# Attention units: the steps of a unit's division spread over ten pairs, a fourth buffer for its sums, routed rows gathered two units ahead, and conversions of `wo` and of the output taken in two pieces

## The chip, the cores and the metric

The kernel runs on one core of a Trainium2 chip. The metric is the device time of one execution in microseconds; the median of 3 runs before the change is 1352.32 us (1351.72 to 1353.39). Engine names are those of the profile: PE (matmuls), PEld (its weight loads), ACT, DVE, POOL, and SP, which here only issues DMAs.

## What is computed

The output is a gated mix of two branches over the same 2048 tokens of width 448: a 16-head attention without a mask (head width 28), and a mixture of 8 experts of which each token takes the best two.

```python
x = A_x
g = _sigmoid((x * gate_w).sum(-1, keepdims=True))
a = _A_ref(x, A_wqkv, A_wo)
b = _B_ref(x, B_w_gate, B_w1, B_w2)
return g * a + (1 - g) * b
```

`_A_ref` is softmax(q k / sqrt(28)) v for each head, then a product with `wo`. `_B_ref` adds, for each expert, its gate weight times silu(x w1) w2.

## The kernel before

The kernel has three stages. The first (to about 116 us of the span) computes q, k, v and the routing. The second (to about 835 us) runs the experts and writes each routed row to the DRAM tensor `ys_d`; PE also takes the row maxima of the scores there. The third, which the change touches, is the attention, followed by the product with `wo`.

The attention runs in 16 units (`NU`): a unit `u` is a group `g` of 4 heads and a block `qc` of 512 queries, `u = 4 g + qc`. A unit is 8 pairs (`NPR`), a pair being two tiles of 128 keys; `m = 8 u + p` counts pairs, 0 to 127. The main loop issues for each `m`, in this order, `scores(m + 1)`, `beside(m)` and `values(m)`. PE, ACT, DVE and POOL run in exactly the order of the code; the DMAs of SP are put in order by a scheduler.

- `scores(m)` takes the scores of a pair on PE into 8 banks of PSUM: for each key tile three heads in a triple `s` and one in a single `z`. ACT turns them into `P` with four exponentials: of the first `z` (L1173), of the first triple (L1174), of the second triple (L1176), and of `X` (L1177), a copy of the second `z` that DVE makes (L1175) so that the bank is free early.
- `values(m)` multiplies `P` with `V` on PE (L1188, 16 matmuls) into a single `z`. DVE adds that to the unit's accumulator `osb` (L1194; at `p == 0` it is a copy, L1192).
- The two singles are used in turn: `values(m)` writes the bank that `scores(m + 1)` used for its first tile, so it waits for L1173; and the last head of the second tile of `scores(m + 2)` goes into the bank of `values(m)`, so PE waits there for DVE's copy or add of `values(m)` into `osb`.
- `beside(m)` holds what is put between the two, and its DVE work stands between the copy `X` of pair `m + 1` and the `osb` step of pair `m`:

```python
        if p in (2, 4, 5, 6):
            next(sums.setdefault(u, routed(u)))
```

  `routed(t)` mixes the two expert rows of each of 128 tokens into `b1`, in four DVE steps (L1073 twice, L1075, L1077); the rows come by `fetch_routed(t)`, two gathers (L1064) that POOL issues, each of 128 rows of 3,584 bytes from `ys_d`. A unit's division (the softmax sums are row 28 of each head in `osb`) takes five steps over DRAM: `collect_sums` (5 DMAs of POOL, the last of which reads the sums back in another layout), `invert_sums` (a reciprocal of DVE and a DMA), `spread_sums` (4 DMAs), `divide` (a DVE product, L1127, and 4 to 8 DMAs of SP into `OT`, L1137). Before, they stand in the next unit at `p` = 0, 3, 4 and 7. In units 4 to 8 the weights `wo` are loaded and converted by `split_wo`; in unit 15 `split_o` converts three tiles of `OT` on DVE (L1086, L180, L181).

After the loop come 16 tiles of the product with `wo` (L1097), each finished by DVE (L1100) and stored by SP; the last unit's division runs beside them.

Of the kernel before, what the change touches and what calls it, by code (L numbers as in the profile page):

```python
# [8 lines left out]
F32 = mybir.dt.float32  # L9
F32R = mybir.dt.float32r  # L10
BF = mybir.dt.bfloat16
I32 = mybir.dt.int32
AF = mybir.ActivationFunctionType
ALU = mybir.AluOpType
# [48 lines left out]
def tile_gated_mha_moe(ctx: ExitStack, tc: tile.TileContext, x, xe_, xT, wv, wqk, wo, w1, w2, out):  # L63
    nc = tc.nc
# [673 lines left out]
    with ExitStack() as pb:  # L738
# [161 lines left out]
        for e in range(E):  # L900
# [12 lines left out]
            for hf in range(2):  # L913
# [75 lines left out]
                for n_k, k in enumerate((4, 0, 1, 2, 3)):  # L989
# [11 lines left out]
                    i = 0  # L1001
# [50 lines left out]
        wo_r[b] = sb.tile([128, D], F32, name="wo_r")  # L1052
        nc.sync.dma_start(wo_r[b], wo[:, b])

    def split_wo(b):
        w_ = wo_r[b]
        nc.vector.tensor_copy(wo_h[:, b], w_)
        nc.vector.tensor_tensor(wo_l[:, b], w_, wo_h[:, b].bitcast(F32), op=ALU.subtract)

    def fetch_routed(t):  # L1060
        yg = []
# [7 lines left out]
    def routed(t):  # L1069
# [7 lines left out]
        nc.vector.scalar_tensor_tensor(b1, yg[1][:, 0], coef[:, 2, t:t + 1], b1, op0=ALU.mult, op1=ALU.add)  # L1077
        yield

    def split_o(t, eng):  # L1080
        ts = slice(t * 128, (t + 1) * 128)
        oh = sb.tile([128, 4, 128], F32R, name="oh", bufs=4)
        if eng is nc.scalar:
            nc.scalar.activation(oh, OT[:, :, ts], AF.Copy)
        else:
            nc.vector.tensor_copy(oh, OT[:, :, ts])  # L1086
        ol = sb.tile([128, 3, 128], F32R, name="ol", bufs=4)
        split_xl(OT[:, :, ts], oh, ol, 128)
        halves[t] = (oh, ol)

    def project(pa_, oh, ol, cs=slice(0, D)):
        mms = []
# [15 lines left out]
    def collect_sums(u):  # L1108
        for j in range(4):
            nc.gpsimd.dma_start(sum_d[u, j:j + 1], accs[u][32 * j + DH:32 * j + DH + 1])  # L1110
        rc[u] = sb.tile([128, 16], F32, name="rc")
        nc.gpsimd.dma_start(rc[u], by_slices(sum_d[u]))

# [66 lines left out]
    def values(m):  # L1180
        u, p = divmod(m, NPR)
        P = Pc.pop(m)
        po = single(m + 1)
        for i in range(2):
            kt = 2 * p + i
            v = held[u // 4][1][kt // 8]
            for j in range(4):
                nc.tensor.matmul(po[32 * j:32 * j + 32], v[:, kt % 8, 32 * j:32 * j + 32], P[4 * i + j],  # L1188
                                 start=i == 0, stop=i == 1)
        if p == 0:  # L1190
            accs[u] = sb.tile([128, 512], F32, name="osb", bufs=3)
            nc.vector.tensor_copy(accs[u], po)  # L1192
        else:
            nc.vector.tensor_tensor(accs[u], po, accs[u], op=ALU.add)  # L1194

    def beside(m):
        u, p = divmod(m, NPR)
        g, qc = divmod(u, 4)
        if qc == 3 and g + 1 < NG:
            if p == 3:  # L1200
                held[g + 1] = [load_k(g + 1, 0), None], [None, None]
            if p == 4:
                held[g + 1][1][0] = load_v(g + 1, 0)
            if p == 6:
                held[g + 1][0][1] = load_k(g + 1, 1)
        if g and qc == 0 and p == 0:
            held[g][1][1] = load_v(g, 1)
        if u and p == 0:
            collect_sums(u - 1)
        if p == 5 and u + 1 < NU:  # L1210
            fetch_routed(u + 1)
        if p == 4 and 4 <= u < 8:
            fetch_wo(u - 4)
        if p == 0 and 5 <= u < 9:
            split_wo(u - 5)
        if (u, p) in WHOLE_O:
            split_o(WHOLE_O.index((u, p)), nc.vector)
        if u and p == 3:
            invert_sums(u - 1)
        if u and p == 4:  # L1220
            spread_sums(u - 1)
        if u and p == 7:
            divide(u - 1)
        if p in (2, 4, 5, 6):
            next(sums.setdefault(u, routed(u)))

    fetch_routed(0)
    WHOLE_O = [(NU - 1, 0), (NU - 1, 1), (NU - 1, 3)]
    for m in range(NU * NPR):
        if m + 1 < NU * NPR:  # L1230
            scores(m + 1)
        beside(m)
        values(m)
    collect_sums(NU - 1)
    split_o(3, nc.scalar)

    for t in range(NT):
# [66 lines left out]
```

## Time and profile before

| | us |
|---|---|
| median of 3 runs | 1352.32 |
| lowest, highest | 1351.72, 1353.39 |
| profiled execution | 1347.44 |
| its span, first to last instruction | 1345.60 |
| attention, first exponential (L1173) to the end of the last values | 835.92 to 1305.9 |
| of it, one pair in the steady part | 3.69 |

The profiled execution is 4.9 us below the median; 1.84 us of it lie outside its span. In the timeline rows each line gives the start, the duration, the engine, the line of the code, the operation with its tiles, how many instructions are merged, and in brackets the idle time of the engine before it and what ended that. ACT starts an instruction before the one ahead of it has ended, so its rate is read from ends (start plus duration), not from durations.

### The profile page before, as it was taken

The page shows a single profiled execution, that of the slowest core. Times are in us where ns is not written, and L with a number is a line of the kernel's source. Part 1 is how long each engine was busy: PE and PEld are TensorE (multiplying, and loading weights), DVE is VectorE, ACT ScalarE, POOL GpSimd, SP SyncE. Part 2 cuts the span into 40 slices and gives each one's busy share as a digit, 9 for nine tenths or more (in the row PEclk, how much of TensorE's full clock was granted, in tenths as well). Part 3 has the DMA queues.
Part 4 walks back from the last instruction along what each step waited for, and adds up shares of the span by engine and source line. Part 5 has one row for each costly group of instructions (what it writes and reads, how often), then busy time and mean ns, then how long its engine had stood idle before and what let it go on. Part 6 is the DMA issues. An engine that isn't in the chain of part 4 may idle for free. (4 is left out here: it accounts for less than half of the span.)

```text
span 1345.6 us, 27214 instructions
## 1 busy us (share of the span) xinstructions
PE 1339.2 (100%) x10166; PEld 888.0 (66%) x10166; DVE 927.7 (69%) x1076; ACT 847.5 (63%) x1270; POOL 617.1 (46%) x661
## 2 busy tenths in 40 slices
PE   9999999999999999999999999999999999999998
PEld 8888788788887777777777777444444444444448
DVE  5736898888988888988898785444454544444465
ACT  5325354364354343543445535999999999999981
POOL 2123765676587577775777753122222222222220
PEclk9999999999999999999999999999999999999999
DMA  9887856753553465534655303223422422342213
GB/s 354 300 266 269 301 154 196 242 153 107 159 157 95 146 201 154 149 101 143 204 156 152 105 36 93 64 58 103 126 83 72 130 80 58 101 126 74 59 31 129
DMA packets 136278, 191.30 MB, mean 142 GB/s; under 512 B 23284, under 2 KB 102680, under 8 KB 135632
## 3 DMA queue, kind: packets, MB, share of 16 engines
q1 hardware_dynamic: 124992, 160.55, 38.6%
q0 software_dynamic: 11008, 28.76, 7.2%
q8 instruction: 80, 1.31, 0.4%
q14 instruction: 54, 0.44, 0.1%
q10 hardware_dynamic: 144, 0.23, 0.1%
HBM read 139.20 MB, written 60.74 MB: 149 GB/s over the span
## 5 line engine op out<-in xcount | busy, mean ns | idle before, releaser
L143 DVE TENSOR_REDUCE mp<-pm 128x3 f32<-128x1536 f32 (+1 forms) x301 | 508.9, 1733 | 11.0 <-PE pm L122 11.0
L1188 PE MATMUL z<-P,V 128*32 128x512 f32 x2032 | 244.7, 598 | 0.1
L1176 ACT ACTIVATE P<-s 128x1536 f32<-128x1536 f32 x127 | 199.2, 1568 | 0.0
L1174 ACT ACTIVATE P<-s 128x1536 f32<-128x1536 f32 x127 | 197.6, 1556 | 0.0
L1175 DVE COPY X<-z 128x512 f32<-128x512 f32 x127 | 87.9, 692 | 150.7 <-PE z L733 141.5
L733 PE MATMUL s<-Q,Kh 29*128 29x512 f32 x1524 | 187.7, 444 | 0.0
L733 PE MATMUL z<-Q,Kh 29*128 29x512 f32 x508 | 185.6, 444 | 0.0
L804 POOL TENSOR_TENSOR w2l<-w2r,w2h 128x448 fp32r<-128x448 f32 x112 | 129.4, 1156 | 119.2 <-ACT w2h L798 80.1
L1020 ACT ACTIVATE yo<-acc 128x448 f32<-128x448 f32 x64 | 34.9, 546 | 233.2 <-PE acc L1006 228.8
L1006 PE MATMUL acc<-w2h,hh 128*128 128x448 f32 x448 | 167.6, 374 | 0.3 <-PEq L818 0.3
L1006 PE MATMUL acc<-w2h,hl 128*128 128x448 f32 x448 | 166.5, 372 | 0.0
L1006 PE MATMUL acc<-w2l,hh 128*128 128x448 f32 x448 | 166.1, 371 | 0.0
L949 ACT ACTIVATE hf<-acc 128x512 f32<-128x512 f32 (+6 forms) x154 | 74.3, 482 | 137.9 <-PE acc L945 131.1
L136 DVE TENSOR_REDUCE mp<-acc 128x1 f32<-128x512 f32 x130 | 89.5, 688 | 85.0 <-PE pm L122 83.1
L813 POOL TENSOR_TENSOR hl<-hf,hh 128x512 fp32r<-128x512 f32 x112 | 145.1, 1295 | 1.0 <-ACT hh L952 1.0
L733 PEld LDWEIGHTS z<-Q,Kh 29*128 29x128 f32 x508 | 74.5, 183 | 106.5 <-DVE yg L1073 26.8
L1188 PEld LDWEIGHTS z<-P,V 128*32 128x32 f32 x2032 | 53.1, 109 | 130.1 <-issue 76.0
L945 PE MATMUL acc<-xeh,w1h 128*128 128x512 f32 (+3 forms) x408 | 136.8, 339 | 0.0
L1194 DVE TENSOR_TENSOR osb<-z,osb 128x512 f32<-128x512 f32 x112 | 77.4, 691 | 85.7 <-PE z L1188 85.6
L945 PE MATMUL acc<-xeh,w1l 128*128 128x512 f32 (+3 forms) x408 | 136.0, 338 | 0.0
L772 POOL TENSOR_TENSOR w1l<-w1r,w1h 128x1024 fp32r<-128x1024 f32 (+1 forms) x49 | 90.8, 1853 | 60.8 <-ACT w1h L766 47.1
L122 PE MATMUL pm<-khg,qg 28*128 28x512 f32 x894 | 110.5, 449 | 0.9 <-DVE lo L645 0.9
(221 smaller groups left out, 2704.7 us busy)
## 6 DMA issues: line engine op xcount, KB each, us to landing
w2r<-in_w_dram SPq DMA_DIRECT2D x112, 224.0 KB
w1r<-in_w_dram SPq DMA_DIRECT2D x56, 384.0 KB
ys_d<-zero_d SPq DMA_DIRECT2D x32, 448.0 KB
ys_d<-yo SPq DMA_DIRECT2D x64, 224.0 KB
x_d<-xf SPq DMA_DIRECT2D x115, 64.0 KB
qkh_d<-hi SPq DMA_DIRECT2D x28, 256.0 KB
qkl_d<-lo SPq DMA_DIRECT2D x28, 256.0 KB
w1r<-in_w_dram SPq DMA_DIRECT2D x112, 64.0 KB
```

The source lines that it names most:

```text
L122: nc.tensor.matmul(banks[n], qgs[g, qt // 4][rw, (qt % 4) * 128:(qt % 4 + 1) * 128], kh[g, kc][rw], start=True, stop=True)
L136: nc.vector.tensor_reduce(mp[:, o:o + 1], banks[0], axis=AX.X, op=ALU.max)
L143: nc.vector.tensor_reduce(mp[:, (o + lo) % 256:(o + lo) % 256 + hi - lo], pm[h][:, lo - 3 * h:hi - 3 * h], axis=AX.X, op=ALU.max)
L733: nc.tensor.matmul(banks[j], k[rw, ks], q[rw, c], start=i == 0, stop=i == 2)
L772: nc.gpsimd.tensor_tensor(l[:, :, half], r[:, :, half], h[:, :, half].bitcast(F32), op=ALU.subtract)
L804: nc.gpsimd.tensor_tensor(w2l, w2r, w2h.bitcast(F32), op=ALU.subtract)
L813: nc.gpsimd.tensor_tensor(hl, hf32, hh[:, 0:512].bitcast(F32), op=ALU.subtract)
L945: nc.tensor.matmul(pu[:, 0:HC], a, b[:, cs], start=i == 0, stop=i == len(mms) - 1)
L1006: nc.tensor.matmul(py[:n, 0:D], a[:, cs], b, start=i == 0, stop=i == 3 * NH - 1)
L1174: nc.scalar.activation(P[:, 1:4], t[0], AF.Exp, scale=SCALE)
L1176: nc.scalar.activation(P[:, 4:7], t[1], AF.Exp, scale=SCALE)
L1188: nc.tensor.matmul(po[32 * j:32 * j + 32], v[:, kt % 8, 32 * j:32 * j + 32], P[4 * i + j], start=i == 0, stop=i == 1)
```

## The change

Of a unit's division, reading the sums back becomes a step of its own (`slice_sums`) at `p == 2` of the next unit, `invert_sums` stays at `p == 3`, `spread_sums` moves to `p == 5`, and `divide` to `p == 2` of the unit after that, so that the division of unit 14 stands behind the loop; `osb` gets 4 buffers instead of 3. `routed(t)` is worked off one unit earlier (at `p` 4 to 7 of unit `t - 1`), for unit 0 at `p` 0 to 3 of unit 0 itself; the gathers of units 0 and 1 are issued ahead of the loop and then those of `u + 2` at `p == 4`. `split_wo` is divided into a rounding at `p == 0` and a subtraction at `p == 1`, and the three `split_o` of unit 15 into two parts each, at `p` 0 and 1, 4 and 5, 6 and 7.

```diff
--- before.py
+++ after.py
@@ -1052,10 +1052,11 @@
         wo_r[b] = sb.tile([128, D], F32, name="wo_r")
         nc.sync.dma_start(wo_r[b], wo[:, b])
 
-    def split_wo(b):
-        w_ = wo_r[b]
-        nc.vector.tensor_copy(wo_h[:, b], w_)
-        nc.vector.tensor_tensor(wo_l[:, b], w_, wo_h[:, b].bitcast(F32), op=ALU.subtract)
+    def split_wo_high(b):
+        nc.vector.tensor_copy(wo_h[:, b], wo_r[b])
+
+    def split_wo_low(b):
+        nc.vector.tensor_tensor(wo_l[:, b], wo_r.pop(b), wo_h[:, b].bitcast(F32), op=ALU.subtract)
 
     def fetch_routed(t):
         yg = []
@@ -1077,16 +1078,19 @@
         nc.vector.scalar_tensor_tensor(b1, yg[1][:, 0], coef[:, 2, t:t + 1], b1, op0=ALU.mult, op1=ALU.add)
         yield
 
+    def split_o_high(t, eng):
+        halves[t] = oh, ol = sb.tile([128, 4, 128], F32R, name="oh", bufs=4), sb.tile([128, 3, 128], F32R, name="ol", bufs=4)
+        if eng is nc.scalar:
+            nc.scalar.activation(oh, OT[:, :, t * 128:(t + 1) * 128], AF.Copy)
+        else:
+            nc.vector.tensor_copy(oh, OT[:, :, t * 128:(t + 1) * 128])
+
+    def split_o_low(t):
+        split_xl(OT[:, :, t * 128:(t + 1) * 128], *halves[t], 128)
+
     def split_o(t, eng):
-        ts = slice(t * 128, (t + 1) * 128)
-        oh = sb.tile([128, 4, 128], F32R, name="oh", bufs=4)
-        if eng is nc.scalar:
-            nc.scalar.activation(oh, OT[:, :, ts], AF.Copy)
-        else:
-            nc.vector.tensor_copy(oh, OT[:, :, ts])
-        ol = sb.tile([128, 3, 128], F32R, name="ol", bufs=4)
-        split_xl(OT[:, :, ts], oh, ol, 128)
-        halves[t] = (oh, ol)
+        split_o_high(t, eng)
+        split_o_low(t)
 
     def project(pa_, oh, ol, cs=slice(0, D)):
         mms = []
@@ -1108,6 +1112,8 @@
     def collect_sums(u):
         for j in range(4):
             nc.gpsimd.dma_start(sum_d[u, j:j + 1], accs[u][32 * j + DH:32 * j + DH + 1])
+
+    def slice_sums(u):
         rc[u] = sb.tile([128, 16], F32, name="rc")
         nc.gpsimd.dma_start(rc[u], by_slices(sum_d[u]))
 
@@ -1188,7 +1194,7 @@
                 nc.tensor.matmul(po[32 * j:32 * j + 32], v[:, kt % 8, 32 * j:32 * j + 32], P[4 * i + j],
                                  start=i == 0, stop=i == 1)
         if p == 0:
-            accs[u] = sb.tile([128, 512], F32, name="osb", bufs=3)
+            accs[u] = sb.tile([128, 512], F32, name="osb", bufs=4)
             nc.vector.tensor_copy(accs[u], po)
         else:
             nc.vector.tensor_tensor(accs[u], po, accs[u], op=ALU.add)
@@ -1207,31 +1213,45 @@
             held[g][1][1] = load_v(g, 1)
         if u and p == 0:
             collect_sums(u - 1)
-        if p == 5 and u + 1 < NU:
-            fetch_routed(u + 1)
+        if u and p == 2:
+            slice_sums(u - 1)
+        if p == 4 and u + 2 < NU:
+            fetch_routed(u + 2)
         if p == 4 and 4 <= u < 8:
             fetch_wo(u - 4)
         if p == 0 and 5 <= u < 9:
-            split_wo(u - 5)
-        if (u, p) in WHOLE_O:
-            split_o(WHOLE_O.index((u, p)), nc.vector)
+            split_wo_high(u - 5)
+        if p == 1 and 5 <= u < 9:
+            split_wo_low(u - 5)
+        if u > 1 and p == 2:
+            divide(u - 2)
         if u and p == 3:
             invert_sums(u - 1)
-        if u and p == 4:
+        if u and p == 5:
             spread_sums(u - 1)
-        if u and p == 7:
-            divide(u - 1)
-        if p in (2, 4, 5, 6):
-            next(sums.setdefault(u, routed(u)))
+        if u == 0 and p < 4:
+            next(first)
+        if p > 3 and u + 1 < NU:
+            next(sums.setdefault(u, routed(u + 1)))
+        if u == NU - 1 and p in AT_O:
+            i = AT_O.index(p)
+            if i % 2:
+                split_o_low(i // 2)
+            else:
+                split_o_high(i // 2, nc.vector)
 
     fetch_routed(0)
-    WHOLE_O = [(NU - 1, 0), (NU - 1, 1), (NU - 1, 3)]
+    fetch_routed(1)
+    first = routed(0)
+    AT_O = (0, 1, 4, 5, 6, 7)
     for m in range(NU * NPR):
         if m + 1 < NU * NPR:
             scores(m + 1)
         beside(m)
         values(m)
     collect_sums(NU - 1)
+    slice_sums(NU - 1)
+    divide(NU - 2)
     split_o(3, nc.scalar)
 
     for t in range(NT):
```

Two places on DVE and one on SP show what moves. DVE at the start of the attention, before (`X`: the copy of the second single, `osb`: the step behind `values`, `yg`: a gathered tile, whose first sum is L1073, L1074 after the change):

```order
L1175 COPY X<-z_9818 128x512
L1192 COPY osb<-z_9837 128x512
L1175 COPY X<-z_9864 128x512
L1194 TENSOR_TENSOR osb<-z_9883,osb 128x512
L1175 COPY X<-z_9909 128x512
L1073 TENSOR_TENSOR yg_9798<-yg_9798 128x448
L1194 TENSOR_TENSOR osb<-z_9930,osb 128x512
```

The same place after the change:

```order
L1181 COPY X<-z_9822 128x512
L1074 TENSOR_TENSOR yg_9798<-yg_9798 128x448
L1198 COPY osb<-z_9843 128x512
L1181 COPY X<-z_9870 128x512
L1074 TENSOR_TENSOR yg_9800<-yg_9800 128x448
L1200 TENSOR_TENSOR osb<-z_9890,osb 128x512
```

The first sum of the gathered rows, which stood ahead of the third `osb` step, now stands ahead of the first. DVE at the start of unit 15, before (`oh` and `ol`: the two parts of a converted tile of `OT`):

```order
L1086 CAST oh<-OT 128x512
L180 TENSOR_TENSOR ol<-OT,oh 128x384
L181 TENSOR_TENSOR oh<-OT,oh 64x128
L1192 COPY osb<-z_15960 128x512
L1175 COPY X<-z_15987 128x512
L1086 CAST oh<-OT 128x512
L180 TENSOR_TENSOR ol<-OT,oh 128x384
L181 TENSOR_TENSOR oh<-OT,oh 64x128
```

and after:

```order
L1086 CAST oh<-OT 128x512
L1198 COPY osb<-z_15952 128x512
L1181 COPY X<-z_15979 128x512
L180 TENSOR_TENSOR ol<-OT,oh 128x384
L181 TENSOR_TENSOR oh<-OT,oh 64x128
L1200 TENSOR_TENSOR osb<-z_16000,osb 128x512
```

Each of the three conversions now has an `osb` step and a copy `X` between its rounding and its subtractions. SP in unit 3, where the keys of the second head group are loaded (`Kh`, `Kl`), before (the four DMAs of a division stand ahead of all of them):

```order
L1137 DMA OT<-osb 28x512 x4
L704 DMA Kh_11166<-qkh_d 28x2x512
L707 DMA Kh_11166<-neg_d 1x1024
L704 DMA Kh_11166<-qkh_d 28x2x512
L707 DMA Kh_11166<-neg_d 1x1024
```

and after:

```order
L704 DMA Kh_11173<-qkh_d 28x2x512
L707 DMA Kh_11173<-neg_d 1x1024
L1143 DMA OT<-osb 28x512 x4
L704 DMA Kh_11173<-qkh_d 28x2x512
L707 DMA Kh_11173<-neg_d 1x1024
```

The four DMAs of a division, which now wait for DVE at `p == 2` of this unit, stand between the first and the remaining loads of the keys.

## Rows read from the trace of the kernel before

**Rows 1.** Part 1 of the page: busy time of each engine, its share of the span, and instructions.

```profile
PE 1339.2 (100%) x10166; PEld 888.0 (66%) x10166; DVE 927.7 (69%) x1076; ACT 847.5 (63%) x1270; POOL 617.1 (46%) x661
```

**Rows 2.** Timeline of one pair in the steady part of the attention (unit 14): ACT, DVE and PE; weight loads and other matmuls left out.

```profile
1267.95 1.56 ACT L1174 ACTIVATE P<-s 128x1536 f32<-128x1536 f32 x1
...
1268.36 0.69 DVE L1175 COPY X<-z 128x512 f32<-128x512 f32 x1 [1.13 <-PE z L733]
...
1269.28 1.58 ACT L1176 ACTIVATE P<-s 128x1536 f32<-128x1536 f32 x1
...
1270.22 0.69 DVE L1194 TENSOR_TENSOR osb<-z,osb 128x512 f32<-128x512 f32 x1 [0.81 <-PE z L1188]
...
1270.61 0.76 ACT L1177 ACTIVATE P<-X 128x512 f32<-128x512 f32 x1
...
1270.96 0.49 PE L733 MATMUL z<-Q,Kh 29*128 29x512 f32 x1
1271.15 0.71 ACT L1173 ACTIVATE P<-z 128x512 f32<-128x512 f32 x1
...
1271.64 1.56 ACT L1174 ACTIVATE P<-s 128x1536 f32<-128x1536 f32 x1
1271.91 1.92 PE L1188 MATMUL z<-P,V 128*32 128x512 f32 x16
```

**Rows 3.** Timeline of the start of the attention: the first `osb` step (838.65), PE's `z` matmul behind it (839.40), the next values (840.30), three of the first four gathers of POOL, and the first sum of gathered rows (844.73).

```profile
838.30 0.96 POOL L1064 DMA_INDIRECT yg<-ys_d,slot_i  x1 [21.45 <-DMA wo_r<-in_wo_dram]
...
838.65 0.69 DVE L1192 COPY osb<-z 128x512 f32<-128x512 f32 x1 [1.32 <-PE z L1188]
...
839.40 0.50 PE L733 MATMUL z<-Q,Kh 29*128 29x512 f32 x1
...
839.56 0.95 POOL L1064 DMA_INDIRECT yg<-ys_d,slot_i  x1 [0.31 <-PE s L733]
...
840.07 1.48 ACT L1174 ACTIVATE P<-s 128x1536 f32<-128x1536 f32 x1
840.30 1.92 PE L1188 MATMUL z<-P,V 128*32 128x512 f32 x16
...
840.81 0.95 POOL L1064 DMA_INDIRECT yg<-ys_d,slot_i  x1 [0.30 <-issue]
...
844.73 0.62 DVE L1073 TENSOR_TENSOR yg<-yg 128x448 f32<-128x448 f32 x1
```

**Rows 4.** The answers for a gathered tile: first two rows for `yg` in the stretch 839.3 to 840.2 (the second gather: instructions with min/median/max ns, then us from issue to landing), the third row the landing of the `xg` gathers of the expert stage (half as many bytes).

```profile
L1064 POOL DMA_INDIRECT yg<-ys_d,slot_i x1: 948/948/948, 839.6 to 839.6; - x1
...
DMA to landing us min/median/max: 4.8/4.8/4.8
...
DMA to landing us min/median/max: 3.6/4.2/7.3
```

**Rows 5.** DMA queues, the queue of the gathers alone: packets, MB, share of 16 engines; first 838.3 to 840, then 840 to 842.

```profile
q0 software_dynamic: 6, 0.04, 13.3%
...
q0 software_dynamic: 82, 0.48, 86.0%
```

**Rows 6.** Timeline of the start of unit 15: the conversion of `OT` in pair 1 (its rounding from 1283.90, the last of its two subtractions to 1285.23), PE's `z` matmul behind it, and the exponential L1174 of the first and of the seventh pair from there.

```profile
1279.01 1.57 ACT L1174 ACTIVATE P<-s 128x1536 f32<-128x1536 f32 x1
...
1283.90 0.43 DVE L1086 CAST oh<-OT 128x512 fp32r<-128x512 f32 x1
...
1284.94 0.29 DVE L181 TENSOR_TENSOR oh<-OT,oh 64x128 fp32r<-64x128 f32 x1
...
1286.00 0.50 PE L733 MATMUL z<-Q,Kh 29*128 29x512 f32 x1
...
1301.47 1.47 ACT L1174 ACTIVATE P<-s 128x1536 f32<-128x1536 f32 x1
```

**Rows 7.** The end: the 8 DMAs of unit 14's division on SP's queue, and the conversion of the first tile that reads them.

```profile
1304.97 6.10 SPq L1137 DMA_DIRECT2D OT<-osb  x8
...
1317.40 0.63 ACT L1084 ACTIVATE oh<-OT 128x512 fp32r<-128x512 f32 x1 [1.61 <-PE s L1097]
```

**Rows 8.** Unit 3 on SP's queue: the 4 DMAs of a division, the last 4 loads of the next group's keys; and PE's first matmul with those keys.

```profile
922.83 3.88 SPq L1137 DMA_DIRECT2D OT<-osb  x4
...
935.33 1.74 SPq L704 DMA_DIRECT2D Kl<-qkl_d  x4
...
949.07 0.49 PE L733 MATMUL z<-Q,Kh 29*128 29x512 f32 x1
```

**Rows 9.** PE's first matmuls (timeline), and two stretches behind its last one (length; busy us of PE, PEld, DVE, ACT, POOL; granted clock as a share of 2.4 GHz; DMA share; GB/s).

```profile
1.55 4.53 PE L376 MATMUL pt<-ident 128*128 128x128 f32 x20 [1.55 <-DVE ident L306]
...
6.64 0.59 PE L371 MATMUL pq<-xel,xh 128*128 128x458 f32 x1
7.02 0.59 PE L371 MATMUL pq<-xeh,xh 128*128 128x458 f32 x1
...
8.27 0.37 PE L371 MATMUL pq<-xel,xh 128*128 128x458 f32 x1
8.48 0.37 PE L371 MATMUL pq<-xeh,xh 128*128 128x458 f32 x1
...
1344.00:1345.00 1.00, 0.00 (x0) 0.00 (x0) 0.00 (x0) 0.00 (x0) 0.00 (x0) 1.00 0.00 0
1345.00:1345.60 0.60, 0.00 (x0) 0.00 (x0) 0.00 (x0) 0.00 (x0) 0.00 (x0) 0.92 0.00 0
```

## The prediction, written before the changed kernel ran

> **What bounds the kernel now.** Read first is part 1 of the page [rows 1]: PE is busy for 100% of the span, ACT for 63%. That does not make PE the bound, since matmul ends are modelled and ACT works little in the two stages ahead of the attention. The change touches the attention alone, so read next is one pair of its steady part [rows 2], on ACT's ends. L1174 ends at 1267.95 + 1.56 = 1269.51, L1176 at 1270.86, L1177 at 1271.37, L1173 at 1271.86 and the next L1174 at 1273.20: steps of 1.35, 0.51, 0.49 and 1.34 us, together 3.69, with no gap between them. ACT is full; 3.69 us is its four exponentials, and neither DVE nor POOL can shorten them. PE follows by a hair: the values begin at 1271.91, 0.05 us after L1173 has ended.
>
> The other thing to see there is the one place where DVE can hold PE up. PE's `z` matmul of the second tile begins at 1270.96, 0.05 us after DVE's `osb` step has ended (1270.22 + 0.69 = 1270.91). That step begins when the values are done, and ahead of it DVE has time: from the end of `X` (1268.36 + 0.69 = 1269.05) to 1270.22, about 1.2 us a pair, of which 0.81 were idle in this one [rows 2]. So DVE work in `beside` costs nothing up to 1.2 us a pair; what is longer, or waits, goes to PE at once and then to ACT.
>
> **What the change can gain.** It must be looked for where DVE passes 1.2 us, and that is only in unit 15, where a whole `split_o` takes from 1283.90 to 1285.23 and PE's `z` slips to 1286.00 [rows 6]. ACT shows the price of all three: L1174 ends at 1279.01 + 1.57 = 1280.58 and six pairs later at 1301.47 + 1.47 = 1302.94, that is 22.36 us for six pairs, where 6 x 3.69 = 22.14. The loss is 0.2 us. In two pieces each conversion fits (0.43 us, then about 0.9), so the gain is 0.2 us; its bounds are 0 and, by PE's own shift in these pairs, 0.5.
>
> The other moves have no wait to remove. `split_wo`, `routed`, `divide` and the reciprocal each fit into their pair before and after. POOL does not stand at the pair where the code places its DMAs: it issued the first gather of unit 1 at 840.81 [rows 3], 1.25 us after the second of unit 0, far ahead of its place at `p == 5`; gathering still earlier frees nobody, and the same holds for reading the sums back, since POOL's DMAs run as soon as what they read is there. The fourth `osb` buffer only makes room for the later `divide`. I cost all of this at nothing; the cover is the 1.2 us of DVE and the eight pairs (29.5 us) that a gather now has.
>
> **What the change costs.** The new wait is at the very start. Before, the first sum of gathered rows ran at 844.73 [rows 3], behind three `X` copies and two `osb` steps. Now it is the first thing behind the first `X` copy, ahead of the first `osb` step. But the first gather is issued at 838.30, because it must wait for the last rows of the experts in `ys_d`, and the change leaves it where it is. The 0.96 us of its row is POOL's part alone. DVE will sit on that landing, behind it the first `osb` copy, and behind that PE's `z` matmul, which ran at 839.40.
>
> The landing of this gather is not shown. Bounds: 4.8 us from issue for the second one, of the same size [rows 4], gives 843.1; the shortest of the `xg` gathers, 3.6 us [rows 4], gives 841.9. Between them the bytes decide: the gather's queue had moved 0.04 MB by 840 and 0.48 MB more by 842 [rows 5]; a gather has 128 x 3,584 bytes = 0.46 MB, so the first was moved at about 841.8, and the second's 0.92 MB some time before its landing at 839.56 + 4.8 = 844.36. I take 4.1 us, 842.4. Then: 842.4 + 0.62 (sum) + 0.69 (`osb` copy) + 0.06 = 843.77 for PE's `z`, against 839.40: **4.4 us** (3.9 to 5.1 by the bounds). The 0.90 us from there to the next values (839.40 to 840.30) stays. ACT has some work left, since L1174 at 840.07 ends at 841.55 and needs nothing of this, but it then stands still, and its next L1173 needs scores that PE only starts after the late values; PE's usual lag behind ACT gives back 0.1 us. I take 4.3 us for ACT, and as ACT is full from there to the end, none comes back.
>
> By the Trainium skill, page "DMA: Bandwidth & Descriptors", section "Anatomy of one DMA — SWDGE (gpsimd) path", such a DMA takes 2.0 us plus its bytes over 436 GB/s, which would be an estimate of 3.05 us, a landing at 841.35 and a sum of about 1355.3 us. The trace has 4.8 us for the second gather, so the page's figure is too small here.
>
> At the group changes SP now puts four DMAs of a division into the loads of the keys: 3.88 us [rows 8]. The last load was issued by 935.33 + 1.74 = 937.07, so by about 941.0 now, and PE needs the keys at 949.07: 8 us are left, more than the longest landing in [rows 4], 7.3. Nothing, at worst 1 us in all three groups.
>
> Behind the loop `divide` of unit 14 comes about 2.3 us later, after the last `osb` step. Its 8 DMAs took 6.10 us from 1304.97 and so end about 1313.4; the conversion that reads them starts at 1317.40 [rows 7]. Nothing.
>
> Sum: 4.3 - 0.2 = +4.1 us. The profiled execution took 1347.44 us with a span of 1345.60, and would take 1351.5 with a span of 1349.7; the median lies 4.9 above the profiled one, and I add the same difference to it: 1352.32 + 4.1 = **1356.4 us**.
>
> **The rivals.** A, the forecast: 1356.4, from 1355.2 to 1357.6 with the bounds of the landing and the scatter of the median (it had 1.7 us between three runs).
>
> B, the stall also costs PE its clock. PE stands for about 4.1 us, from the end of the three matmuls ahead of `z` to 843.8. At the end of the span, behind the last matmul, the mean granted clock is 1.00 over 1344 to 1345 and 0.92 over 1345.00 to 1345.60 [rows 9], so with PE idle it fell there from 2.4 to 1.2 GHz. At the start matmuls follow one another in 0.38 us (6.64 to 7.02) and later in 0.21 (8.27 to 8.48), the low level and the high; with the first matmul at 1.55, PE ran at the low level for up to 5.9 us [rows 9]. At half speed PE cannot keep up with ACT, so a fall would cost up to half of that, 3.0 us, and I take 2.2: 1358.6. For it: PE idles here much as it does at the end. Against it: no row shows a fall between two matmuls, and whether the clock falls in a pause of this length may differ between executions. The Trainium skill, page "TensorE: Matmul & The Clock Gate", section "HAM oscillation — how this bites in real kernels", speaks against the change here: pauses of PE between bursts throttle it, at a price of the throttled time times one half. The end of this trace agrees with the fall; what one costs inside the kernel no row shows.
>
> C, the other side: the stall is earned back. Pairs would then run at less than 3.69 us, because PE and not ACT sets the pace and goes faster once it is late. At the 0.05 us by which PE lags behind ACT [rows 2] it needs 4.1 / 0.05 = 82 of the 126 pairs, and would give 1352.3 with all of it back. Against it: ACT's ends, which leave no gap [rows 2], and the 0.2 us of unit 15, which were not earned back either.
>
> D, the gather is no wait, since what it waits for at 838.30 comes earlier, or DVE reaches it later: then only the gain is left, 1352.1. It would need a landing by 838.65 - 0.62 = 838.0, ahead of its issue.
>
> E, the keys or the late `divide` come too late after all: 1357.5 and more.
>
> **How the numbers follow.** A 0.67, B 0.21, C 0.04, D 0.03, E 0.05. The range reaches from a little below A to most of B: 1354.7 to 1359.4. About 0.2% (2.7 us) is what a measurement can tell from no change, so below 1349.6 is faster, above 1355.0 slower. Faster 0.01; same C, D and a small part of A with a short landing, 0.10; slower 0.89.
>
> **What would show it.** In the changed profile the first sum of gathered rows should start at 842 to 843, as the wait of DVE for a DMA, the first `osb` copy behind it, PE's `z` at 843.5 to 844.5; ACT should have one gap of about 4 us there, and then steps of 3.69 to the end. L1174 should need 22.1 us for the six pairs of unit 15. The granted clock in the pairs behind the stall decides between A and B. I am wrong if the first `osb` copy runs before 840 as it did, if pairs after the stall take less than 3.69, or if PE waits for keys at a group change.

## The result, and the profile after

The changed kernel takes **1361.09 us** (median of 5 runs, 1360.22 to 1361.58) where the kernel before takes 1353.39 beside it (1351.72 to 1355.16): a ratio of 1.0052 [1.0041, 1.0063]. That is 7.7 us between the medians and 7.0 by the ratio. The forecast was 1356.4, 4.1 us slower, with a range up to 1359.4: the right sign, too small a size.

In what follows the *stretch* runs from the first exponential of the attention to the first product matmul; the *start* is the first 8 pairs, counted from ACT's first triple of exponentials (that of pair 1, since pair 0's scores are taken earlier by another line); the *loop* is the next 112 pairs, up to unit 15; then come six pairs of unit 15. All are differences of row starts.

The timeline of the start after the change, answering to [rows 3]; L1074, L1198, L1194 and L1180 are the old L1073, L1192, L1188 and L1174. The attention begins at 839.24 in this profile and at 835.92 in that of before, so all times lie 3.3 us later:

```profile
842.01 0.96 POOL L1065 DMA_INDIRECT yg<-ys_d,slot_i  x1 [21.88 <-DMA wo_r<-in_wo_dram]
...
842.57 0.50 PE L733 MATMUL s<-Q,Kh 29*128 29x512 f32 x3
...
846.25 0.62 DVE L1074 TENSOR_TENSOR yg<-yg 128x448 f32<-128x448 f32 x1 [5.60 <-DMA yg<-ys_d,slot_i]
846.80 0.68 DVE L1198 COPY osb<-z 128x512 f32<-128x512 f32 x1
847.53 0.79 PE L733 MATMUL z<-Q,Kh 29*128 29x512 f32 x1 [4.46 <-DVE yg L1074]
...
848.81 1.45 ACT L1182 ACTIVATE P<-s 128x1536 f32<-128x1536 f32 x1 [3.95 <-PE s L733]
849.11 3.14 PE L1194 MATMUL z<-P,V 128*32 128x512 f32 x16
...
853.96 1.07 PE L1194 MATMUL z<-P,V 128*32 128x512 f32 x8
```

This is the forecast wait, step by step: the gather is issued at 842.01, the sum that waits for its landing starts 4.24 us later, then come the `osb` copy and `z`; PE's idle time ahead of `z` is 4.46 us. The 16 value matmuls behind it take 3.14 us instead of 1.92. The stretches say why (length; busy us of PE, PEld, DVE, ACT, POOL; granted clock; DMA share; GB/s):

```profile
842.00:844.00 2.00, 1.08 (x15) 0.42 (x11) 0.00 (x0) 2.00 (x4) 1.69 (x2) 1.00 0.37 57
844.00:846.00 2.00, 0.00 (x0) 0.00 (x0) 0.00 (x0) 0.86 (x1) 1.39 (x3) 0.69 0.79 265
846.00:848.00 2.00, 0.47 (x4) 0.47 (x8) 1.23 (x2) 0.00 (x0) 0.72 (x1) 0.50 0.89 315
848.00:850.00 2.00, 2.00 (x17) 0.60 (x17) 0.73 (x2) 1.19 (x1) 0.00 (x0) 0.50 0.74 283
850.00:852.00 2.00, 2.00 (x16) 0.35 (x8) 0.49 (x1) 0.78 (x2) 0.00 (x0) 0.60 0.05 15
852.00:854.00 2.00, 2.00 (x32) 1.25 (x30) 0.69 (x1) 0.76 (x2) 0.00 (x0) 1.00 0.00 0
```

PE fell from 2.4 to 1.2 GHz while it stood, and ran its next pair at half speed: rival B. The granted clock is 0.69 in the stretch in which PE did nothing, 0.50 behind it and 1.00 again from 852. The start takes 36.0 us where the first profile of before has 29.4.

A second loss was in no part of the prediction. Once in nearly every unit, where POOL gathers, a pair and the one behind it take longer (3.86 and 3.89 us in unit 1, from L1180 to L1180, instead of 3.69). Unit 1 after the change:

```profile
889.19 1.01 POOL L1065 DMA_INDIRECT yg<-ys_d,slot_i  x1 [0.31 <-issue]
...
889.98 0.71 ACT L1179 ACTIVATE P<-z 128x512 f32<-128x512 f32 x1
...
890.37 0.39 PE L733 MATMUL z<-Q,Kl 28*128 28x512 f32 x1
890.47 1.56 ACT L1180 ACTIVATE P<-s 128x1536 f32<-128x1536 f32 x1
890.50 0.97 POOL L1065 DMA_INDIRECT yg<-ys_d,slot_i  x1 [0.30 <-issue]
...
891.47 2.07 POOL L1128 DMA_DIRECT2D rs<-inv_d  x4
...
892.03 0.69 DVE L1181 COPY X<-z 128x512 f32<-128x512 f32 x1 [2.29 <-ACT P L1180]
...
892.78 0.49 PE L733 MATMUL z<-Q,Kh 29*128 29x512 f32 x1
```

The last matmul into the second `z` ends at 890.37 + 0.39 = 890.76, yet `X`, which reads it, starts at 892.03; 2.05 us behind L1179, where it is otherwise 0.9. The next `z` of PE waits for `X`. The row gives ACT's L1180 as what ended DVE's wait, but that is inferred, and DVE waits here on PE's semaphore. Among the trace's semaphore updates, PE's own for this `z` stands at 891.94, 1.18 us behind the matmul's end; usually it follows at 0.01. By the Trainium skill, page "Perfetto Trace Analysis", section "Tensor Engine Instruction (MATMUL, LD_WEIGHTS)", the end of a matmul in a profile is an estimate, and the update leaves when PSUM has acknowledged the write; no row here shows that acknowledgement. I call this a **late signal**. The expectations below count updates over 0.25 us behind that end (42 of 641 in this loop, 0 of 631 in the first profile of before); such counts are too high, since near gathers some updates have no record and the next is taken for them. So the table below counts late `X` copies, those of the loop that start over 1.3 us behind their pair's first exponential (the median is 0.89): 14 of 112 after the change, all in pairs with gathers or the pair behind, and none in the first profile of before. Unit 15 is as forecast: the ends of L1180 now lie 1316.59 - 1294.47 = 22.12 us apart for the six pairs of [rows 6], 22.36 there:

```profile
1292.91 1.56 ACT L1180 ACTIVATE P<-s 128x1536 f32<-128x1536 f32 x1
...
1315.03 1.56 ACT L1180 ACTIVATE P<-s 128x1536 f32<-128x1536 f32 x1
```

### The profile page after: what moved, and what is told of

Same layout as the page of the kernel before. It is cut to its first block, busy times and chain, and to the rows that moved or that the text cites. A ratio compares the mean times of both kernels' runs of the same rounds, so it can differ in the third digit from the quotient of the medians.

```text
span 1359.3 us, 27197 instructions
## 1 busy us (share of the span) xinstructions
PE 1343.4 (99%) x10166; PEld 891.6 (66%) x10166; DVE 925.1 (68%) x1076; ACT 849.8 (63%) x1270; POOL 616.3 (45%) x661
## 5 line engine op out<-in xcount | busy, mean ns | idle before, releaser
L1194 PE MATMUL z<-P,V 128*32 128x512 f32 x2032 | 245.9, 601 | 0.1
L1182 ACT ACTIVATE P<-s 128x1536 f32<-128x1536 f32 x127 | 193.1, 1521 | 4.1 <-PE s L733 4.0
L1180 ACT ACTIVATE P<-s 128x1536 f32<-128x1536 f32 x127 | 192.5, 1516 | 0.0
L1194 PEld LDWEIGHTS z<-P,V 128*32 128x32 f32 x2032 | 53.3, 109 | 129.0 <-issue 77.9
L1114 POOL DMA_DIRECT2D sum_d<-osb x64 | 31.0, 493 | 186.4 <-DVE osb L1200 186.4
```

The lines of the kernel that those rows point to most:

```text
L1180: nc.scalar.activation(P[:, 1:4], t[0], AF.Exp, scale=SCALE)
L1182: nc.scalar.activation(P[:, 4:7], t[1], AF.Exp, scale=SCALE)
```

## Experiments

Fifteen runs on three chips: e1 to e4 on one, e5 to e7 on a second, e8 to e15 on a third. Between chips the kernel before differs by about as much as the change costs. Chip and sitting can't be told apart for the first two; the third was used in two sittings (e8 to e11, e12 to e15) and had late signals in both. Us, from each profile; the last column is the median, and in brackets that of the kernel before on the same chip:

```
                            late X   start   loop  unit 15  stretch  time (before)
before, first profile          0     29.39  413.21  22.47   469.9    1347.44 (one)
after, first profile          14     36.00  417.19  22.11   480.2    1361.09 (1353.39)
e1  first steps at p 2, 3     12     32.82  417.52  22.13   477.4    1356.08 (1353.75)
e2  rs ahead of gathers       12     35.97  414.46  22.12   477.5    1358.48 (1353.75)
e3  e1 and e2                 12     32.79  415.24  22.14   475.1    1355.32 (1353.75)
e4  PE kept at work           14     35.22  416.96  22.12   479.2    1359.03 (1353.75)
e5  before                     0     29.37  412.95  22.46   469.6    1346.64 (1346.78)
e6  before, gathers first      0     29.39  413.22  22.45   469.9    1346.55 (1346.78)
e7  before, first sum early    0     36.97  412.95  22.48   477.2    1353.12 (1346.78)
e8  before                    13     31.10  413.87  22.45   472.3    1352.99 (1354.21)
e9  after                     14     36.55  416.83  22.12   480.4    1360.29 (1354.21)
e10 = e1                      12     33.03  417.08  22.14   477.2    1357.66 (1354.21)
e11 first steps from p 1      12     31.16  417.68  22.14   475.9    1357.11 (1354.21)
e12 plain rows, POOL           0     29.37  412.95  22.12   469.4    1349.22 (1352.99)
e13 plain rows, SP             0     30.47  412.93  22.11   470.4    1350.26 (1352.99)
e14 = e6                      14     30.98  415.82  22.43   474.1    1354.26 (1352.99)
e15 e11 and e2                12     32.72  414.28  22.11   474.1    1354.27 (1352.99)
```

**e1.**

```diff
-        if u == 0 and p < 4:
-            next(first)
+        if u == 0 and p in (2, 3):
+            next(first)
+            next(first)
```

> Undoes one part: in unit 0 the four steps on gathered rows stand at p 2 and 3, two in each, and not at p 0 to 3; all else as after the change. From the first exponential of the attention to the first product of the last stage the profile of before has 470.0 us, that of after 480.2. Theory: 6.7 of the 10.3 us are the start, 4.8 as the wait for the first gather and 1.9 as the half clock behind it. Then the first values follow without a wait, the granted clock stays at 1.00, the stretch takes 473.5 us and the time is about 1354.4. Rival 1: the wait only moves, to p 2, since the gathers land no earlier; the first sum then starts at 846 as before, but with two osb steps ahead of it, and less than 3 us come back: 477 to 479. Rival 2: the clock falls without the wait; about 5 come back: 475.4. The late X copies, one a unit, are to stay in all three.

Ratio 1.0017 [1.0008, 1.0026]. The start gave back 3.2 us, not 6.7: it still has a late signal in the middle of the four gathers, and the clock fell once, for a shorter time. So the forecast wait explains only part of the start on this chip. This late signal holds up two engines:

```profile
841.47 0.40 PE L733 MATMUL s<-Q,Kl 28*128 28x512 f32 x3
...
844.28 1.45 ACT L1182 ACTIVATE P<-s 128x1536 f32<-128x1536 f32 x1 [0.96 <-PE z L1194]
844.38 0.69 DVE L1181 COPY X<-z 128x512 f32<-128x512 f32 x1 [3.38 <-PE z L1194]
```

ACT stands 0.96 us for a triple whose last matmul had ended at 841.87, and PE's update stands at 844.26. So it is PE's signal that is late, and not DVE that is held up beside POOL.

**e2.** `spread_sums(u - 1)` moved from `p == 5` to `p == 4`, ahead of the gathers.

> Undoes another part: the four DMAs that spread the sums (rs) stand ahead of the two gathers on POOL, both at p 4; the start is as after the change. Theory: the loss of about 0.3 us at one pair of each of the units 1 to 13 (X begins 1.2 us late there, 12 times) comes from the gathers standing between the write of the reciprocals and rs; then every X comes 0.4 us behind L1179 and the stretch takes 480.2 - 3.7 = 476.5 us, the time about 1357.4. Rival 1: it comes from what else moved in these pairs, above all the OT DMAs of a division on SP since p 2, or the sums read back at p 2; then X stays late and nothing comes back: 480.2, 1361. Rival 2: the gathers alone make X late, wherever they stand, when X falls into their time; then it also shows here, now at the place of the gathers: 479 to 480.2.

1.0035 [1.0023, 1.0047]. The loop gave back 2.7 us, but `X` is still late at the gathers' new place, in half of the units by less (1.5 us behind the first exponential instead of 2.1). Both the theory (the order) and rival 2 (the gathers wherever they stand) are right in part.

**e3.** e1 and e2 together.

> Both of the two changes above: steps of unit 0 at p 2 and 3, and rs ahead of the gathers. Theory: what is left of the change is the gain of 0.2 us in unit 15, so 470.0 - 0.2 = 469.8 us for the stretch and a time of 1352 to 1353, the same as before within 0.1%. Rival: another cost of the change is hidden under the first two (keys, the late division, the fourth buffer); then the stretch takes over 470.5 us, and the waits show where.

1.0010 [1.0001, 1.0019]. The time was nearly that of before, but the stretch was 5.3 us longer than theory said. Either a third cost was hidden, or the first profile of before was no measure for this chip; e5 and e8 ask which.

**e4.** In `scores(2)`, ahead of the second tile's passes:

```diff
+            if m == 2 and i:
+                for _ in range(7):
+                    for j in range(3):
+                        rw = slice(32 * j, 32 * j + KR)
+                        nc.tensor.matmul(three[j], held[0][0][0][0][rw, kt * 128:(kt + 1) * 128], qs[u][rw, 0], start=True, stop=True)
```

> As after the change, with the wait left in place, but TensorE kept at work through it: ahead of the waiting z matmul the first score pass of the same tile's three other banks is written 7 times more (21 matmuls, 4.5 us at 0.21), each overwritten by the next. Theory: the wait of 4.8 us stays, the clock stays at 1.00, and the 1.9 us of slow matmuls come back: 478.3 us, about 1359.2. Rival 1: the slow matmuls cost nothing, since ACT is behind anyway: 480.2, 1361. Rival 2: the granted clock falls all the same, since it isn't the pause that lowers it: 480.2 with a row of 0.50 behind the wait.

1.0039 [1.0023, 1.0054]. Mis-sized: the 21 matmuls took 1.7 us (841.14 to the next pass at 842.85), not 4.5, since the three of a pass run beside one another (three take 0.40 us there, one 0.39). PE still stood 2.32 us, the clock still fell, but for less of the time:

```profile
844.00:846.00 2.00, 0.43 (x8) 0.39 (x9) 1.23 (x2) 0.00 (x0) 0.89 (x1) 1.00 0.93 312
846.00:848.00 2.00, 2.00 (x21) 0.52 (x17) 1.22 (x2) 1.63 (x2) 0.00 (x0) 0.68 0.77 298
848.00:850.00 2.00, 2.00 (x16) 0.34 (x9) 0.05 (x1) 0.33 (x1) 0.00 (x0) 0.50 0.09 33
850.00:852.00 2.00, 1.98 (x28) 1.28 (x32) 0.86 (x2) 0.98 (x2) 0.00 (x0) 0.96 0.00 0
```

The start gave back 0.8 us, 0.5 of it because the gather landed sooner behind the first exponential. The rest does not settle the price of the clock.

**e5.** The kernel before, unchanged.

> The kernel before once more, for a second profile of it. In the profile of before not one of 625 signals of PE (a matmul's last update of its semaphore) comes over 0.25 us after the matmul's end; in that of after 42 of 624 do, all of them while POOL issues gathers, by 0.5 to 2.1 us; the X copies that are late, one a unit, wait for these. Theory: this lag belongs to the gathers and not to the change, and the first profile of before (1347.44, 4.3 us under the quickest of the timed runs) is one without it. Then this profile shows late signals at the gathers too, some of the X copies late, the stretch from the first exponential to the first product at 473 to 477 us and not 470, and a time of 1351 to 1357. Rival: the lag comes with the change (rows gathered two units ahead, a fourth buffer); then no signal is late here, the stretch has 470 us, and the 4 to 6 us by which the timed runs are slower than the first profile lie ahead of the attention.

0.9997 [0.9988, 1.0007]. No late `X`, and all its runs took 1346 to 1348. Neither theory nor rival: this chip is a quick one. The first profile of before agrees with it (stretch 469.9 against 469.6, no late `X`), so most likely it came from such a chip.

**e6.** In the kernel before, `fetch_routed(u + 1)` at `p == 4` instead of 5, which puts POOL's gathers ahead of `rs`.

> The kernel before with one part of the change alone: the next unit's gathers at p 4, ahead of the spreading of the sums, so that POOL issues reciprocals, gathers, rs as after the change. Theory: signals of PE are late at the gathers, and as this order puts the gathers 0.79 us ahead of an L1173 in each unit, X is late in nearly every unit and 0.25 to 0.3 us are lost each time: 3 to 4 us over the stretch without any late X, 474 to 480 with what the first gathers cost at the start. Rival: the order is nothing, and the stretch is that of the kernel before on the same chip within 1 us.

0.9998 [0.9989, 1.0008]. Without late signals the order is worth nothing that can be measured (0.3 us of loop).

**e7.** In the kernel before:

```diff
-        if p in (2, 4, 5, 6):
+        if p in ((2, 4, 5, 6) if u else (0, 1, 2, 3)):
             next(sums.setdefault(u, routed(u)))
```

> The kernel before with another part of the change alone: in unit 0 the four steps on gathered rows stand at p 0 to 3 and not at 2, 4, 5 and 6. Theory: the wait of DVE for the first gather (landing 4.1 to 4.3 us behind its issue) stands ahead of the first osb copy, PE waits 4 to 5 us, the granted clock falls to 0.50 behind it for some us, and the start (first triple of exponentials to that of the second unit) has 35 to 36 us where an undisturbed one has 29.4 and one with only late signals about 32.8; so the time is 3 us above the kernel before if its runs have the late signals, 6.5 above if they don't. Rival: the wait is there but the pairs behind it make it good; then the start has under 33 us.

1.0044 [1.0027, 1.0060], 6.3 us: the wait and the half clock by themselves, on a chip with no late signal. Its timeline, then its stretches:

```profile
838.27 0.96 POOL L1064 DMA_INDIRECT yg<-ys_d,slot_i  x1 [21.74 <-PE z L1188]
...
842.48 0.63 DVE L1073 TENSOR_TENSOR yg<-yg 128x448 f32<-128x448 f32 x1 [5.42 <-DMA yg<-ys_d,slot_i]
...
843.76 0.79 PE L733 MATMUL z<-Q,Kh 29*128 29x512 f32 x1 [4.28 <-DVE osb L1192]
...
845.33 3.64 PE L1188 MATMUL z<-P,V 128*32 128x512 f32 x16
```

```profile
842.00:844.00 2.00, 0.24 (x4) 0.24 (x8) 1.23 (x2) 0.00 (x0) 0.95 (x1) 0.88 0.90 323
844.00:846.00 2.00, 2.00 (x13) 0.79 (x17) 0.51 (x1) 0.97 (x1) 0.00 (x0) 0.50 0.78 290
846.00:848.00 2.00, 2.00 (x16) 0.39 (x8) 0.71 (x2) 1.00 (x2) 0.00 (x0) 0.50 0.09 26
848.00:850.00 2.00, 2.00 (x20) 0.92 (x16) 0.69 (x1) 0.00 (x0) 0.00 (x0) 0.50 0.00 0
```

`z` comes 8.12 us behind the first exponential (835.64) and not 3.48 [rows 3]: a wait of 4.6. The start is 7.6 us longer, so the clock cost 3.0 in this run, the slowest of the four; with the same wait, the 6.3 us of the median leave 1.7.

**e8.** The kernel before, on the third chip.

> The kernel before a third time, as the profile beside the next three. So far two chips were seen: one on which signals of PE are late at gathers (after 42 of 641 in the loop, the four experiments on it 32 to 44; its runs of the kernel before took 1351 to 1357), and one on which none is (before twice, 0 of 631; 1346 to 1348). Theory: the chip decides, not the kernel. If this chip is of the first kind, this profile of the kernel before shows late signals, 25 or more, late X copies, and a stretch of 473 to 477 us; if of the second, none and 469.8. Rival: late signals come only with kernels that have the change; then a profile of before on the first kind of chip has none and 470 us.

0.9996 [0.9987, 1.0005]. The theory holds, with the stretch (472.3) a little under its range: 13 late `X` copies in the kernel before. The same place in unit 1:

```profile
887.28 1.02 POOL L1064 DMA_INDIRECT yg<-ys_d,slot_i  x1 [0.30 <-issue]
...
888.30 0.72 ACT L1173 ACTIVATE P<-z 128x512 f32<-128x512 f32 x1
...
888.61 0.97 POOL L1064 DMA_INDIRECT yg<-ys_d,slot_i  x1 [0.30 <-issue]
...
888.70 0.38 PE L733 MATMUL z<-Q,Kl 28*128 28x512 f32 x1
...
890.16 0.69 DVE L1175 COPY X<-z 128x512 f32<-128x512 f32 x1 [2.09 <-PE z L733]
...
890.92 0.49 PE L733 MATMUL z<-Q,Kh 29*128 29x512 f32 x1
```

`X` comes out 2.88 us behind the first gather's issue, as after the change (892.03 - 889.19 = 2.84). But here L1173 starts 1.02 us behind that issue, there 0.79. After the change 11 of the 12 late copies right at the gathers lie 2.84 to 3.03 us behind the first issue, here ten of twelve 2.88 to 2.93, and in e2 half lie at 2.9 and half at 2.1. So the gathers, for the most part, fix when `X` comes; the order fixes how late that is for its pair: 0.95 us here, 1.15 after.

**e9.** The changed kernel on the same chip.

> The changed kernel once more, beside a profile of the kernel before on the same chip. Theory: its loss is the wait for the first gather (4.4 to 4.8 us) and the half clock behind it (about 2), less 0.2 in unit 15. On a chip without late signals that is all: a start (first triple to that of unit 1) of 36 us where before has 29.4, pairs of 3.69 to the end, the stretch 470 + 6.5 = 476.5 and the time 6.3 to 6.8 above before. On a chip with late signals the loop (8 to 120) has 417.2 and before has 1 to 3 us less, and the start of before is itself longer, 32 to 33: 6 to 8 above before. Rival: the gathers ahead of rs cost 3.7 us on any chip; then the loop is 417 also without late signals, and the time 10 above.

1.0046 [1.0032, 1.0061]. Against e8 the stretch is 8.2 us longer: start +5.4, loop +3.0, unit 15 -0.3. The start of before is itself 1.7 us longer here than on the quick chip, so less of the wait and the clock shows in the difference.

**e10.** As e1.

> The changed kernel with the four steps of unit 0 at p 2 and 3 again. Theory: without late signals there is no wait left, the granted clock stays at 1.00, and the time is that of the kernel before less 0.2 us (within 0.5 us of it). With late signals it stays about 2 above it. Rival: something else of the change costs time, keys or the late division: 1 us or more above before also without late signals.

1.0026 [1.0017, 1.0036]. The case with late signals, but 3.5 us above before and not 2.

**e11.** In place of e1's condition: `0 < p < 4`, with two steps at `p == 3`.

> The changed kernel with the steps of unit 0 one pair later only: p 1, 2, 3 and 3. The first sum stands behind the first osb copy, 2 to 3.7 us later than after the change, so without late signals about 1 us of the wait is left or less (the gather lands 6.5 to 7 us behind the first exponential, and DVE comes there at about 5.2). Theory: the wait shrinks by the 3.7 us of a pair and PE's pause with it, the clock does not fall, and the start is 30 to 31 us where the change has 36. Rival: the clock falls also behind a pause of 1 to 1.5 us; then the start has 32 to 33 us with a row at 0.50.

1.0024 [1.0015, 1.0033]. The first sum follows `X` with no wait for the gather, and the clock holds:

```profile
846.39 0.69 DVE L1181 COPY X<-z 128x512 f32<-128x512 f32 x1 [3.37 <-PE z L1194]
847.00 0.61 DVE L1074 TENSOR_TENSOR yg<-yg 128x448 f32<-128x448 f32 x1
```

```profile
846.00:848.00 2.00, 0.87 (x15) 0.70 (x15) 1.35 (x3) 1.69 (x2) 0.72 (x1) 1.00 0.84 287
848.00:850.00 2.00, 1.73 (x24) 0.67 (x21) 0.87 (x2) 1.80 (x2) 0.00 (x0) 1.00 0.82 288
```

In this profile the start, 31.16 us, is that of e8 (31.10): one pair later, and the whole cost of the start is gone. What is left, 3 to 4 us, is the loop. Not every execution keeps its clock, though: e15 has the same start and lost it.

**e12 and e13.** The gather by index replaced, on POOL (`gpsimd`) and on SP (`sync`):

```diff
-            nc.gpsimd.indirect_dma_start(out=..., in_=ys_d, in_offset=...)
+            nc.gpsimd.dma_start(y.rearrange("p c d -> p (c d)"), ys_d[t * 128:t * 128 + 128])
```

(The first line is shortened.) Both kernels leave out the choice of the rows: each DMA takes 128 rows in order.

> The changed kernel with its gathers replaced by plain DMAs of the same size on the same queue of POOL (each takes 128 rows in order and not by index, so the choice of the rows is left out; these rows are written earlier, so the wait at the start should go too). Theory: on a chip with late signals they belong to the gather by index, as POOL works on it. Then no signal of PE is late in the loop, no X is late, the start has about 29.4 us, the loop 8 to 120 about 413.0 and the time is 1346 to 1349 on any chip. Rival 1: any DMA of this size from POOL's queue does it, by what it moves or by the descriptors that POOL writes: then 30 or more signals are late and the loop stays at 417 on such a chip. Rival 2: it is what stands around the gathers in these pairs; then too.

> The same with the plain DMAs on SP's queue, so that POOL has no part in them. Theory: no late signals, loop 413.0, as on POOL's queue. If the run before has late signals and this one none, POOL's work on a DMA of this size is the cause and not the index; if both have them, it is the 0.46 MB that are written to SBUF, or the pairs themselves.

Ratios 0.9973 [0.9962, 0.9984] and 0.9981 [0.9972, 0.9991]. On a chip with late signals the attention now has none, and its loop is that of e5. So they belong to the gather by index, not to the bytes moved, POOL's queue (between 880 and 1275 us it moved 15.94 MB in e12, 15.67 after the change) or the pairs around it. Whether it is the work on the indices or the scattered rows, no run tells apart. Who waits for `X` between 880 and 1275 us (us, times), after the change and in e12, where nobody does:

```profile
who waited for it (us, times):
  PEld z L733: 13.3, 12
  PE z L733: 2.0, 9
```

```profile
L1180 DVE COPY X<-z x107: 691/692/693, 882.8 to 1273.6; 128x512 f32<-128x512 f32 x107
...
who waited for it (us, times):
busy tenths in 40 slices 0000000000000000000000000033333433333300
```

**e14.** As e6, now on a chip with late signals.

> The kernel before with the gathers ahead of rs once more; the first time no signal was late on that chip, and the order cost nothing (stretch 469.92 against 469.64). Theory: on a chip with late signals the order has a price: the first signal lies 0.79 us behind the gather's issue and not 1.05, X and the next triple come later, and the loop 8 to 120 takes 416.5 to 417.5 where before has 413.9 there; the time is 2.5 to 3.5 above before. Rival: the loop stays at 413.9, and the 3 us more of the changed kernel come from its other moves.

1.0008 [0.9999, 1.0018]. The loop takes 1.9 us more than in e8: the order alone has a price here, under the expected one. It is two thirds of the 3.0 us of e9; from which other move the rest comes was not settled.

**e15.** e11 and e2 together.

> What the runs point to: the changed kernel with the steps of unit 0 at p 1, 2, 3 and 3 (start 31.2 us on a chip with late signals, as in the kernel before) and rs ahead of the gathers (loop 414.5 to 415.2). Theory: the stretch is 471.5 to 473.5 on such a chip, where before has 472.3, and 469.5 on one without late signals, where before has 469.7: the same as the kernel before within 0.1%, since unit 15 gives only 0.2 to 0.3 us. Rival: steps closer together at the start make the clock fall here: 475 or more.

1.0010 [1.0001, 1.0018]. Loop and unit 15 as expected, and 2.5 of the 3.0 us of loop are back (414.28 against 416.83 in e9). But the clock fell in the start all the same: 0.67 over 848 to 850 and 0.50 over 850 to 852, and a start of 32.72 us. In unit 0 the order of this kernel is that of e11, where it held at 1.00, so this is a difference between executions. PE's longest pauses there were 0.98 us in e15, 1.15 in e11 and 1.17 in e1, where it also fell.

The mean granted clock of the single runs says the same of the kernel before: of its 28 runs beside e8 to e11, 15 have 0.996 or 0.997 and take 1353.95 to 1355.97 us, 11 have 0.999 or 1.000 and take 1351.27 to 1354.17. It, too, loses its clock in about half of its executions on this chip, by these numbers, though where in the run isn't on record. All nine runs of the changed kernel (five in the result, four in e9) have 0.996 or 0.997. No version that takes the right rows beat the kernel before.

## Why the prediction was wrong

The sign came from the step that was forecast, the wait at the start; the size was missed by two costs that its sum doesn't hold, PE's clock and the late signals in the loop. On the third chip, where both kernels were profiled, the start costs 5.4 us against the 4.3 forecast, the loop 3.0 against nothing, and unit 15 gives back 0.3 against 0.2. There the loop is the larger part of the miss; in e7, on a chip without late signals, the clock is.

- **Bound and gain: right.** ACT's 3.69 us a pair hold wherever signals come on time (112 pairs in 413 us), and unit 15 gave its 0.2 us (0.24 by the ends of the triples; the table goes by starts and has 0.35). Rivals C, D and E did not occur: no pair ran faster to earn anything back, and PE waited for no keys.
- **The wait: right, a little small.** 4.4 us forecast, 4.6 in e7 and 4.8 after (847.53 - 839.24 = 8.29 us, less the 3.48 of before; the gather's issue slipped by 0.4). The landing was taken as 4.1 us; the sum that waits for it starts 4.24 us behind the issue, 4.21 in e7. The formula of the Trainium skill, page "DMA: Bandwidth & Descriptors", section "Anatomy of one DMA — SWDGE (gpsimd) path", gives an estimate of 3.05 us; the measurement decides.
- **First step that failed: "no row shows a fall between two matmuls", and so A at 0.67 over B at 0.21.** The clock fell in every profile in which the first sum waited at `p == 0` for its gather (after, e2, e4, e7, e9), on all chips. Its price, taken as 2.2 us, was 36.0 - 29.4 - 4.8 = 1.8 after, counted from an undisturbed start, and 3.0 in the profile of e7. The rule of the Trainium skill, page "TensorE: Matmul & The Clock Gate", section "HAM oscillation — how this bites in real kernels", that pauses between bursts throttle PE, agrees with these traces (0.50 behind a pause of 4.46 us). Behind pauses of about 1 us the clock fell in some profiles (e1, e15) and held in others (e8, e11). On a chip without late signals B is nearly the whole result: 6.3 us in e7.
- **Second: "I cost all of this at nothing", of POOL's order.** That holds where signals are on time (e6). In the changed kernel's profile of the comparison, and on the chip of e8 to e15, PE's signals are late at the gathers, and putting them ahead of `rs` moves them 0.2 to 0.3 us earlier against the pair: 1.9 us by e14 of the 3.0 in the loop. The trace I had could not show it.
- **Third, the one that could have warned: "the median lies 4.9 above the profiled one, and I add the same difference to it".** That was no scatter between runs of one chip. e5 and e8, the same kernel on two chips, differ by 6.35 us; the profiles find 5.8 of it: the first exponential at 838.76 instead of 835.56 (3.2; the stages ahead of it gather by index too, but what costs them this was not looked into), the start 1.7, the loop 0.9. A change to the gathers can change such a difference.

What stays open: why PE's signals come late on some chips while POOL works on a gather by index and not on others, what decides whether the clock falls behind a short pause, and about 1 us of the changed kernel's loop.

## What to carry to other kernels

Before a step is moved to the front of an engine's order, look at when its data can be there: at the front the step cost PE 4.6 us and then its clock; one pair later it was free in one profile (e11) and cost 1.6 us in another (e15), in which the clock fell. A pause of PE inside a kernel is to be priced with its clock. And when a profiled execution is quicker than all timed runs, the difference is a part of the kernel that this profile doesn't show: find it, or take the profile from the chip of the timing.

## What was unexpected of the hardware

PE's semaphore updates came up to 2.4 us after the matmul's end (in e1 at 844.26 for one that ended at 841.87) around gathers by index on two of the three chips of the experiments, while the matmuls right behind them started on time: the values in unit 1 after the change began at 890.74, on time, and signalled at 892.71, on time. On the other chip the largest such lag in the attention was 0.05 us. The kernel before takes 1346.6 us there and 1353 to 1354 on the others.
